# Where a weight conversion keeps its low word, and when half of a folded matrix leaves PSUM

## Chip, cores and metric

The kernel runs on one core of a Trainium2 chip. The metric is device microseconds (us) of one execution, as the median of three runs. TensorE multiplies matrices into PSUM (8 banks), VectorE and ScalarE work on SBUF and PSUM, GpSimd works on SBUF alone, and SyncE issues most DMAs. In the rows below PE is TensorE, DVE VectorE, ACT ScalarE, POOL GpSimd and SP SyncE.

## What is computed

Three stages in a row: an attention over keys and values that are pooled by 8, a bilinear layer with float64 weights, and a mixture of 8 experts with one expert for each token.

```python
k_p = k.reshape(B, H, Sp, pool, D).mean(axis=3)      # v_p likewise; pool = 8
attn = softmax(scale * q @ k_p.T);  x = attn @ v_p    # 4608 tokens x 512
a, b = x @ w1, x @ w2                                 # float64 weights, 512 x 1024
x = ((a * b) @ w3) @ w_out                            # 1024 x 1024, 1024 x 512
e = argmax(x @ w_gate + modality_bias[modality_id])   # one expert of 8
out = gate * relu(x @ ew1[e]) @ ew2[e]
```

## The kernel before

Every float32 matrix product is made of three passes over a high and a low part (`mm3`, lines 113 to 116). The float64 weights are loaded as raw 64-bit words, in pieces of 128x512 (512 KB), and turned into such a pair by `conv` (line 388). A conversion is a chain of six instructions. ScalarE makes two 32-bit words, the high one `m` (line 391) and the low one `t` (line 393), in the two halves of one SBUF tile `scr`. VectorE joins them in two operations (lines 394 and 395), each with both tensor inputs `m` and `t`. ScalarE rounds the result into the high part (line 396), and GpSimd subtracts that from it into the low part (`sub_pool`, line 119). There are 40 conversions: 24 for the fold, 16 for w1 and w2.

The **fold** computes w3 @ w_out once, as W (1024x512), in two passes of eight steps of 12 matmuls. The first pass takes a conversion of w_out and one of the first half of w3 for each step (16 in all), into four PSUM banks `accs` (the tag "mm"). The second takes one conversion a step, of the second half of w3, into `accs2`: the two banks of the tag "sc" and the two of the tag "tp". The first four attention tiles (`softmax_tile`, `attn_T`, `attn_V`, and `prep_v1` with the pooled values) run between the steps of the first pass. Then `fold_out` copies both halves out of PSUM as a high and a low part, on ScalarE (line 439) and VectorE (line 440), and `prep_w12(m)` converts piece m of w1 and w2. Pieces 0 and 1 come before the first chunk and pieces 2 to 7 in it, two conversions for each of the eight steps m of `mm1`, where attention tiles 4 to 7 run too. Their scores go to the tag "sc".

Values are summed by 8 in `pool_sum` (line 153), as one VectorE reduction (line 155) or as three additions on GpSimd (`tree_sum`, line 150). For batch 0, pieces 3 to 5 go to VectorE and pieces 0 to 2 to GpSimd; batch 1 is VectorE's; later batches are GpSimd's.

Raw pieces of the fold pass through a ring of 11 places. Places 0 to 3 lie in the SBUF of the tag "Wh" and places 4 to 7 in that of "Wl", so a tile of W in "Wh" cannot be written before the last conversion has read places 0 to 3. `fold_load` issues load n once conversion n - 11 is done.

The order of the work up to the end of the first chunk is made by the compiler's planner from the order in which the program is written and from its own estimate of when each instruction is ready. From the second chunk on the order is the written one. Each engine runs its own instructions in order.

Of the kernel before, what the change touches and what calls it, by code (L numbers as in the profile page):

```python
# [10 lines left out]
F32, F32R, BF16, I32, U32, I64, U16 = dt.float32, dt.float32r, dt.bfloat16, dt.int32, dt.uint32, dt.int64, dt.uint16  # L11
AF = mybir.ActivationFunctionType
ALU = mybir.AluOpType
# [9 lines left out]
P = 128  # L23
NT = N // P
NC_ = N // 512
SUM_V = (3, 4, 5)
IDC_M = 2
ACT_T, MM_T = (0, 1, 2, 4, 5, 6, 7), (1, 3)
V_POOL = 2
# [50 lines left out]
def flat(ap):  # L80
    return ap.rearrange("p a b -> p (a b)")
# [8 lines left out]
def _program(outer, tc, nc, I, out):  # L90
    def pool(stack, name, bufs=1, **kw):
        return stack.enter_context(tc.tile_pool(name=name, bufs=bufs, **kw))
# [3 lines left out]
    wp = pool(outer, "wp")  # L96
# [4 lines left out]
    def mm_ps(name, shape=(P, 512)):  # L101
        return psum.tile(list(shape), F32, name=name, tag="mm", bufs=4)

    def tp_ps(name, shape=(P, 512)):
        return psum.tile(list(shape), F32, name=name, tag="tp", bufs=2)

    def st4(name, shape, dtype):
        return st.tile(list(shape), dtype, name=name, tag="st4", bufs=6)

    def st2(name, shape=(P, 512), dtype=F32):  # L110
        return st.tile(list(shape), dtype, name=name, tag="st2", bufs=2)

    def mm3(ps, wh, wl, xh, xl, start, stop):
        nc.tensor.matmul(ps, lhsT=wh, rhs=xh, start=start, stop=False)  # L114
        nc.tensor.matmul(ps, lhsT=wh, rhs=xl, start=False, stop=False)  # L115
        nc.tensor.matmul(ps, lhsT=wl, rhs=xh, start=False, stop=stop)  # L116

    def sub_pool(lo, f, hi):
        nc.gpsimd.tensor_tensor(lo, f, hi.bitcast(F32), op=ALU.subtract)  # L119
# [28 lines left out]
    def tree_sum(out, t):  # L148
        for w in (4, 2, 1):
            nc.gpsimd.tensor_tensor(out if w == 1 else t[:, :, :w], t[:, :, 0] if w == 1 else t[:, :, :w],  # L150
                                    t[:, :, 1] if w == 1 else t[:, :, w:2 * w], op=ALU.add)

    def pool_sum(out, t, j, b):
        if 0 < b < V_POOL or b == 0 and j in SUM_V:
            nc.vector.tensor_reduce(out=out, in_=t, op=ALU.add, axis=AX.X)
            return
        tree_sum(out, t)
# [52 lines left out]
    def early_v(b):  # L210

        if b < B and b not in v_raw:
            pairs = [st4("vr2", (P, 2, D, POOL), F32) for _ in range(3)]
            v_raw[b] = [pairs[j // 2][:, j % 2] for j in range(6)]
            for j in range(6):
                load_v(b, j, v_raw[b][j])
# [167 lines left out]
    def load64(src, raw):  # L384
        nc.sync.dma_start(raw, src)
        return raw

    def conv(raw, hi, lo):
        s = st4("scr", (P, 2, 512), I32)
        f, m, t = s[:, 0].bitcast(F32), s[:, 0], s[:, 1]  # L390
        nc.scalar.activation(f, raw.bitcast(F32)[:, 1::2], AF.Copy, scale=float(2.0 ** -112))

        nc.scalar.activation(t, raw.bitcast(U32)[:, 0::2], AF.Copy, scale=TOP_S, bias=TOP_B)
        nc.vector.scalar_tensor_tensor(out=t, in0=m, scalar=3, in1=t, op0=ALU.logical_shift_left, op1=ALU.bitwise_or)
        nc.vector.scalar_tensor_tensor(out=m, in0=m, scalar=-2147483648, in1=t, op0=ALU.bitwise_and, op1=ALU.bitwise_or)
        nc.scalar.copy(hi, f)  # L396
        sub_pool(lo, f, hi)

    def run(hooks, n):
        for f in hooks.get(n, ()):  # L400
            f()
# [6 lines left out]
    ring = [x[:, i] for x in [wp.tile([P, 4, 512], I64, name="stage", tag=tag) for tag in ("Wh", "Wl")] for i in range(4)]  # L408
# [7 lines left out]
    order = [x for j in range(8) for x in (("wo", j), ("w3", j, 0))] + [("w3", j, 1) for j in range(8)]  # L416
    raws = {}

    def fold_load():
        n = len(raws)  # L420
        if n < len(order):
            k = order[n]
            raws[k] = load64(I[k[0]][k[1:]], ring[n % len(ring)])

    def fold_conv(k):
        dst = wos[k[1]] if k[0] == "wo" else w3s[k[1]]
        conv(raws[k], dst[:, 0], dst[:, 1])
        fold_load()

    def fold_mm(accs, j):  # L430
        w3, wo = w3s[j].rearrange("p t (k n) -> p t k n", k=4), wos[j]
        for k in range(4):
            mm3(accs[k], w3[:, 0, k], w3[:, 1, k], wo[:, 0], wo[:, 1], j == 0, j == 7)

    def fold_out(accs, h):

        for k in range(4):
            kb = 4 * h + k
            nc.scalar.copy(Wh[:, kb], accs[k])
            nc.vector.tensor_tensor(Wl[:, kb], accs[k], Wh[:, kb].bitcast(F32), op=ALU.subtract)  # L440

    names = ("w1h", "w1l", "w2h", "w2l")
    wt12 = []
    raw12 = {}
# [3 lines left out]
    def load_w12(m):  # L448
        if m < 8 and m not in raw12:
            raw12[m] = [load64(I[n][m], cv[:, 2 * (m % 2) + i]) for i, n in enumerate(("w1", "w2"))]  # L450

    def prep_w12(m):
        if m < 8 and m == len(wt12):
            load_w12(m)
            t = w12.tile([P, 4, 4, P], F32R, name=f"w{m}", tag=w_tag(m), bufs=1)
            wt12.append({n: t[:, i] for i, n in enumerate(names)})
            for i in range(2):
                conv(raw12[m][i], flat(t[:, 2 * i]), flat(t[:, 2 * i + 1]))
            load_w12(m + 2)

    att = Attention(0)
# [14 lines left out]
    accs = [mm_ps("wps") for _ in range(4)]  # L476
    for j in range(8):
        if j < 4:
            att.S(j)
        if j == 4:  # L480
            att.V1()
        if j == 5:
            sct = psum.tile([P, 2, 512], F32, name="sct", tag="sc", bufs=1)
            att.T((0, 1), {0: sct[:, 0], 1: sct[:, 1]})
            att.T((2, 3))
        if j == 6:
            sct = psum.tile([P, 2, 512], F32, name="sct", tag="sc", bufs=1)
            att.T((4,), {4: sct[:, 0], 5: sct[:, 1]})
        for k in order[2 * j:2 * j + 2]:
            fold_conv(k)  # L490
        fold_mm(accs, j)
    att.V()
    x_first = att.x
    sc = psum.tile([P, 2, 512], F32, name="wps3", tag="sc", bufs=1)
    accs2 = [sc[:, 0], sc[:, 1]] + [tp_ps("wps2") for _ in range(2)]
    load_w12(0)
    load_w12(1)
    for j in range(8):
        fold_conv(order[16 + j])
        fold_mm(accs2, j)  # L500
    prep_w12(0)
    Wh = wp.tile([P, 8, 512], F32R, name="Wh", tag="Wh")
    Wl = wp.tile([P, 8, 512], F32R, name="Wl", tag="Wl")
    fold_out(accs, 0)
    fold_out(accs2, 1)
    W = (Wh, Wl)
    prep_w12(1)


    def prep_routing():  # L510
# [44 lines left out]

    def mm_w(ch, ab, hooks, W, x2s, amid=None):
        abh, abl = ab
        Wh, Wl = W
        for i in range(4):
            t = 4 * ch + i  # L560
            cols = slice(P * i, P * i + P)
            ps = mm_ps("x2ps")
            for m in range(8):
                for l, r in ((abh, Wh), (abh, Wl), (abl, Wh)):
                    nc.tensor.matmul(ps, lhsT=l[:, m, cols], rhs=r[:, m], start=m == 0 and r is Wh and l is abh, stop=m == 7 and l is abl)  # L565
                if amid and i == 0 and m == 3:
                    amid()
            if i == 2:
                pair = st4("x2b", (P, 2, 512), F32)
            x2 = st2("x2") if i < 2 else pair[:, i - 2]  # L570
            nc.scalar.copy(x2, ps)
            nc.sync.dma_start(x2d[P * t:P * t + P, :], x2)
            x2s.append(x2)
            run(hooks, i)
# [67 lines left out]

    def first_chunk():
        att = Attention(1)
        h1 = {m: [lambda m=m: prep_w12(m + 2)] for m in range(8)}
        h1[0] += [lambda: att.K(0)]
        for i in range(4):
            h1[i + 1] += [lambda i=i: att.S(i)]
        h1[4] += [lambda: early_v(1)]
        h1[6] += [att.V1, lambda: att.T((0, 1))]  # L650
        h1[7] += [lambda: att.T((2, 3)), lambda: load_k(2), lambda: att.T((4,))]
        ab = mm1(0, x_first, h1)
        wgb = wp.tile([P, E, 512], F32, name="wgb", tag="wgb")
        nc.sync.dma_start(wgb, I["wgt"].partition_broadcast(P))
        return att, ab, wgb
# [4 lines left out]

    def next_chunk(ch, x, W, old):
        att = Attention(ch + 1)
# [8 lines left out]
        ab = mm1(ch, x, h1)  # L671
        mm_w(ch, ab, tail_hooks(ch, x2s, b, att), W, x2s)
        old_ent[:] = [sc[0][2]]
# [4 lines left out]
    x2s = []  # L678
    mm_w(0, ab, tail_hooks(0, x2s, 2, att1), W, x2s)
    x_cur = att1.x  # L680
    with tc.manual_schedule(engines={ET.PE, ET.DVE, ET.Activation, ET.Pool, ET.SP}):
        for ch in range(1, NC_ - 1):
            x_cur, x2s = next_chunk(ch, x_cur, W, x2s)
    def experts(x, old):
# [352 lines left out]
```

## Time and profile before

| | us |
|---|---|
| median of three runs (1221.94 to 1223.17) | 1222.15 |
| the profiled execution | 1223.66 |
| its span, first to last instruction | 1221.6 |
| TensorE busy in the span | 1166.5 |
| VectorE busy | 809.1 |
| ScalarE busy | 495.7 |
| GpSimd busy | 313.5 |

The profile was read in this order: the busy time of each engine, its slices in time, the waits of TensorE, and then the timelines of the other engines around those waits. An idle time in a row stands in brackets or behind the last bar, with what ended it. A busy TensorE is not one at full clock, so the granted clock (PEclk) is read beside it. A matmul's row is longer than its pitch, since neighbours overlap.

### The profile page before, as it was taken

Reading aid. Unit: us, or ns where it says so; the run is one execution under the profiler, and the core shown is the slowest. Engines: PE = TensorE matmul, PEld = TensorE weight load, DVE = VectorE, ACT = ScalarE, POOL = GpSimd, SP = SyncE. Lnnn points to the kernel's source line nnn. Section 1 sums busy time; section 2 is a strip of 40 time slices with the busy share of each in tenths; the row PEclk is TensorE's granted clock in tenths of the full one; section 3 lists DMA queues with packets and bytes.
Section 4 is the critical chain, followed back from the end, with each engine's and each line's share of the span. In section 5 each row is a group of like instructions: output and inputs, shape, how many; then the busy total and the mean of one; then the engine's idle time right before and its main releaser. Section 6 shows DMA issues by size and latency. Waiting matters only on the chain. (4 is left out here: it accounts for less than half of the span.)

```text
span 1221.6 us, 16215 instructions
## 1 busy us (share of the span) xinstructions
PE 1166.5 (95%) x5458; PEld 969.9 (79%) x5458; DVE 809.1 (66%) x1758; ACT 495.7 (41%) x967; POOL 313.5 (26%) x420
## 2 busy tenths in 40 slices
PE   4698899999999999999999999989999999999988
PEld 3466788888888888888888888868888888888867
DVE  6799787688687886877767684784444444445452
ACT  6587732222323223232232222713545545545452
POOL 3665501503315033150331101112121212122120
PEclk9899899999999999999999999989999999999998
DMA  9636332121121211211101000607645655654750
GB/s 334 205 139 221 133 114 72 48 76 43 57 91 48 73 45 56 91 48 71 47 18 36 1 35 17 217 10 266 182 129 182 192 144 172 208 156 131 203 149 18
DMA packets 89426, 136.68 MB, mean 112 GB/s; under 512 B 49304, under 2 KB 49560, under 8 KB 89176
## 3 DMA queue, kind: packets, MB, share of 16 engines
q1 hardware_dynamic: 82088, 115.72, 29.8%
q0 software_dynamic: 7232, 19.71, 5.0%
q8 instruction: 47, 0.77, 0.3%
q14 instruction: 59, 0.48, 0.1%
HBM read 106.26 MB, written 20.55 MB: 104 GB/s over the span
## 5 line engine op out<-in xcount | busy, mean ns | idle before, releaser
L114 PE MATMUL w<-xh,w 128*128 128x512 f32 x576 | 230.5, 400 | 3.7 <-ACT w L396 3.7
L116 PE MATMUL w<-xh,w 128*128 128x512 f32 x576 | 226.1, 392 | 1.4 <-POOL w L119 1.4
L115 PE MATMUL w<-xl,w 128*128 128x512 f32 x576 | 225.2, 391 | 0.0
L295 POOL TENSOR_TENSOR ex<-ex,sm 128x576 f32<-128x576 f32 x35 | 40.9, 1167 | 375.1 <-DVE sm L289 287.6
L114 PEld LDWEIGHTS w<-xh,w 128*128 128x128 f32 x576 | 108.9, 189 | 25.7 <-ACT w L396 4.1
L116 PEld LDWEIGHTS w<-xh,w 128*128 128x128 f32 x576 | 108.8, 189 | 25.8 <-POOL w L119 2.5
L115 PEld LDWEIGHTS w<-xl,w 128*128 128x128 f32 x576 | 109.0, 189 | 21.3
L764 DVE SCALAR_TENSOR_TENSOR abl<-e,abh 128x512 fp32r<-128x512 f32 (+2 forms) x80 | 51.8, 650 | 102.2 <-ACT abh L763 100.7
L114 PE MATMUL e<-e,abh 128*128 128x512 f32 x296 | 115.4, 390 | 0.5 <-ACT e L719 0.5
L115 PE MATMUL e<-e,abh 128*128 128x512 f32 x296 | 115.3, 390 | 0.2 <-DVE e L720 0.2
L116 PE MATMUL e<-e,abl 128*128 128x512 f32 x296 | 115.2, 389 | 0.0
L565 PE MATMUL x2ps<-Wh,abh 128*128 128x512 f32 x288 | 113.4, 394 | 0.8 <-DVE xl L324 0.8
L551 ACT CAST abh<-asb 128x512 fp32r<-128x512 f32 x72 | 44.7, 620 | 167.8 <-DVE asb L550 167.8
L565 PE MATMUL x2ps<-Wh,abl 128*128 128x512 f32 x288 | 112.4, 390 | 0.0
L565 PE MATMUL x2ps<-Wl,abh 128*128 128x512 f32 x288 | 112.3, 390 | 0.0
L777 POOL DMA_INDIRECT out<-o,idc x37 | 42.0, 1136 | 255.3 <-ACT o L776 143.0
L579 DVE CUSTOM_DVE_ANT_0 junk<-x2b,wgb,bias 128x512 f32<-128x512 f32 x144 | 102.3, 766 | 0.0
L579 DVE CUSTOM_DVE_ANT_0 junk<-x,wgb,bias 128x512 f32<-128x512 f32 x144 | 99.2, 755 | 0.2
L114 PE MATMUL e<-xh,e1h 128*128 128x512 f32 (+2 forms) x240 | 91.9, 383 | 5.6 <-DVEq L976 4.7
L550 DVE TENSOR_TENSOR asb<-asb,w 128x512 f32<-128x512 f32 x72 | 49.4, 685 | 66.2 <-PE w L116 31.1
L115 PE MATMUL e<-xl,e1h 128*128 128x512 f32 (+2 forms) x240 | 91.3, 380 | 0.0
L116 PE MATMUL e<-xh,e1l 128*128 128x512 f32 (+2 forms) x240 | 91.2, 380 | 0.0
(209 smaller groups left out, 2323.8 us busy)
## 6 DMA issues: line engine op xcount, KB each, us to landing
raw<-ew_in SPq DMA_DIRECT2D x80, 512.0 KB
q<-q_in SPq DMA_DIRECT2D x36, 256.0 KB
cv<-w_in SPq DMA_DIRECT2D x16, 512.0 KB
kr<-k_in SPq DMA_DIRECT2D x28, 288.0 KB
vr<-v_in SPq DMA_DIRECT2D x28, 256.0 KB
stage<-w_in SPq DMA_DIRECT2D x12, 512.0 KB
x2d<-x SPq DMA_DIRECT2D x18, 256.0 KB
x2d<-x2b SPq DMA_DIRECT2D x18, 256.0 KB
```

The source lines that it names most:

```text
L114: nc.tensor.matmul(ps, lhsT=wh, rhs=xh, start=start, stop=False)
L115: nc.tensor.matmul(ps, lhsT=wh, rhs=xl, start=False, stop=False)
L116: nc.tensor.matmul(ps, lhsT=wl, rhs=xh, start=False, stop=stop)
L295: eng.tensor_tensor(e3, e3, bc(sm.unsqueeze(2), [P, H, SP_]), op=ALU.mult)
L550: nc.vector.tensor_tensor(a, a, ps[1], op=ALU.mult)
L551: nc.scalar.copy(abh[:, m], a)
L565: nc.tensor.matmul(ps, lhsT=l[:, m, cols], rhs=r[:, m], start=m == 0 and r is Wh and l is abh, stop=m == 7 and l is abl)
L579: nc.vector.tensor_tensor_reduce(out=junk[e % 2], in0=x2s[i], in1=wgb[:, e], scale=1.0, scalar=bias[:, 4 * ch + i, e:e + 1], op0=ALU.mult, ...
L764: nc.vector.scalar_tensor_tensor(out=hT[1][:, m, :w], in0=ps[:, :w], scalar=0.0, in1=hT[0][:, m, :w].bitcast(F32), op0=ALU.max, op1=ALU.su ...
L777: nc.gpsimd.indirect_dma_start(out=out, out_offset=bass.IndirectOffsetOnAxis(idc[:, i, 0:1], 0), in_=o, in_offset=None, bounds_check=N - 1 ...
```

## The change

- `pool_sum` sends all six pieces of batch 0 to VectorE.
- `conv` takes `ps_of`, a maker of PSUM tiles. With it, the low word `t` lies in a PSUM bank and `m` stays in the SBUF tile. The fold's second pass uses it from step 2 on and `prep_w12(0)` and `prep_w12(1)` do, with the four "mm" banks; `prep_w12(2)` to `prep_w12(7)` use the two "tp" banks. That is 6 + 16 = 22 of the 40 conversions.
- `fold_out` for the first half (`accs`) runs in two parts behind steps 0 and 1 of the second pass, into a tile of its own in "Wh". The second half follows `prep_w12(1)`, into a tile in "Wl". W becomes a list of eight pairs.
- The last two raw loads of the fold (22 and 23) go to places 4 and 5 of the ring in place of 0 and 1, and are issued behind conversions 15 and 16 where they were behind 11 and 12.

```diff
     def pool_sum(out, t, j, b):
-        if 0 < b < V_POOL or b == 0 and j in SUM_V:
+        if b < V_POOL:
             nc.vector.tensor_reduce(out=out, in_=t, op=ALU.add, axis=AX.X)
...
-    def conv(raw, hi, lo):
-        s = st4("scr", (P, 2, 512), I32)
-        f, m, t = s[:, 0].bitcast(F32), s[:, 0], s[:, 1]
+    scr = []
+
+    def conv(raw, hi, lo, ps_of=None):
+        if len(scr) < 2:
+            s = st4("scr", (P, 2, 512), I32)
+            scr[:] = [s[:, 1], s[:, 0]]
+        m = scr.pop()
+        f, t = m.bitcast(F32), ps_of("low").bitcast(I32) if ps_of else scr.pop()
+        if len(scr) == 1 and not ps_of:
+            scr.clear()
...
-            raws[k] = load64(I[k[0]][k[1:]], ring[n % len(ring)])
+            raws[k] = load64(I[k[0]][k[1:]], ring[n % len(ring) if n < 22 else n - 18])
+
+    convs = []
...
-        conv(raws[k], dst[:, 0], dst[:, 1])
-        fold_load()
+        conv(raws[k], dst[:, 0], dst[:, 1], ps_of)
+        convs.append(k)
+        if len(raws) < 22 or len(convs) >= len(raws) - 6:
+            fold_load()
...
-    def fold_out(accs, h):
-        for k in range(4):
-            kb = 4 * h + k
-            nc.scalar.copy(Wh[:, kb], accs[k])
-            nc.vector.tensor_tensor(Wl[:, kb], accs[k], Wh[:, kb].bitcast(F32), op=ALU.subtract)
+    def fold_out(accs, w, ks):
+        for k in ks:
+            nc.scalar.copy(w[:, 0, k], accs[k])
+            nc.vector.tensor_tensor(w[:, 1, k], accs[k], w[:, 0, k].bitcast(F32), op=ALU.subtract)
+            W.append((w[:, 0, k], w[:, 1, k]))
...
+    W = []
+    w0 = wp.tile([P, 2, 4, 512], F32R, name="W0", tag="Wh")
...
     for j in range(8):
-        fold_conv(order[16 + j])
+        fold_conv(order[16 + j], mm_ps if j > 1 else None)
         fold_mm(accs2, j)
-    prep_w12(0)
-    Wh = wp.tile([P, 8, 512], F32R, name="Wh", tag="Wh")
-    Wl = wp.tile([P, 8, 512], F32R, name="Wl", tag="Wl")
-    fold_out(accs, 0)
-    fold_out(accs2, 1)
-    W = (Wh, Wl)
-    prep_w12(1)
+        if j < 2:
+            fold_out(accs, w0, (2 * j, 2 * j + 1))
+    prep_w12(0, mm_ps)
+    prep_w12(1, mm_ps)
+    fold_out(accs2, wp.tile([P, 2, 4, 512], F32R, name="W1", tag="Wl"), range(4))
...
-        h1 = {m: [lambda m=m: prep_w12(m + 2)] for m in range(8)}
+        h1 = {m: [lambda m=m: prep_w12(m + 2, tp_ps)] for m in range(8)}
```

## Rows read from the trace of the kernel before

**Rows 1.** Windows: stretch, length, then busy us of each engine (with counts), clock, DMA
```profile
155.00:1221.60 1066.60, 1048.59 (x4975) 879.28 (x4973) 683.94 (x1582) 388.61 (x696) 229.79 (x340) 0.99 0.32 99
```

**Rows 2.** Waits of PE, 15 to 155 us: total us, times, longest
```profile
PE wps L115 <- POOL f L119: 4.0, 1, 4.0
PE sc L265 <- ACT ex L280: 3.8, 1, 3.8
PE w L114 <- ACT w L396: 3.7, 1, 3.7
PE wps L116 <- POOL f L119: 3.4, 5, 1.3
PE w L116 <- POOL w L119: 1.4, 2, 0.9
```

**Rows 3.** Timeline of POOL, first pass: start, us, line, count, idle before
```profile
36.13 2.05 POOL L150 TENSOR_TENSOR earlyabl<-earlyabl 128x256 f32<-128x256 f32 x2
...
42.57 1.27 POOL L119 TENSOR_TENSOR f<-scr,f 128x512 fp32r<-128x512 f32 x1
```

**Rows 4.** Timelines of ACT and DVE, first pass
```profile
42.65 0.91 ACT L234 ACTIVATE vbh<-vs,c 128x256 fp32r<-128x256 f32 x2 [2.79 <-POOL vs L150]
...
54.80 0.59 ACT L305 CAST f<-sct 128x512 fp32r<-128x512 f32 x1 [5.48 <-PE sct L304]
...
43.19 1.33 DVE L235 SCALAR_TENSOR_TENSOR vbl<-vs,c,vbh 128x256 fp32r<-128x256 f32 x2 [1.68 <-ACT vbh L234]
...
55.42 0.69 DVE L306 TENSOR_TENSOR f<-sct,f 128x512 fp32r<-128x512 f32 x1 [2.63 <-ACT f L305]
```

**Rows 5.** Windows around three waits, and one without: columns PE, PEld, DVE, ACT, POOL, clock
```profile
43.90:52.70 8.80, 7.54 (x17) 5.47 (x18) 8.74 (x13) 4.69 (x10) 5.37 (x5) 0.51 0.70 243
77.00:94.00 17.00, 17.00 (x76) 14.07 (x75) 16.18 (x17) 13.85 (x26) 10.21 (x7) 1.00 0.28 85
106.80:110.40 3.60, 3.08 (x7) 2.03 (x8) 3.60 (x5) 3.60 (x8) 3.46 (x3) 0.55 0.03 14
125.70:131.30 5.60, 5.57 (x17) 4.86 (x18) 5.57 (x10) 4.55 (x9) 3.75 (x3) 0.52 0.26 91
```

**Rows 6.** Groups of DVE, 76.5 to 140 us: count, busy us, mean ns, idle before
```profile
L395 DVE SCALAR_TENSOR_TENSOR scr<-scr 128x512 int32<-128x512 int32 x21 | 20.9, 1008 | 0.2
L394 DVE SCALAR_TENSOR_TENSOR scr<-scr 128x512 int32<-128x512 int32 x21 | 20.4, 985 | 0.6 <-ACT scr L393 0.6
L440 DVE TENSOR_TENSOR Wl<-wps,Wh 128x512 fp32r<-128x512 f32 x8 | 5.0, 679 | 0.0
L552 DVE TENSOR_TENSOR abl<-asb,abh 128x512 fp32r<-128x512 f32 x4 | 3.6, 894 | 0.0
L550 DVE TENSOR_TENSOR asb<-asb,w 128x512 f32<-128x512 f32 x4 | 2.7, 676 | 0.0
L155 DVE TENSOR_REDUCE vs<-vr 128x64 f32<-128x512 f32 x4 | 2.7, 663 | 0.0
```

**Rows 7.** Groups of DVE, whole span: one that writes PSUM
```profile
L579 DVE CUSTOM_DVE_ANT_0 junk<-x,wgb,bias 128x512 f32<-128x512 f32 x144 | 99.2, 755 | 0.2
```

**Rows 8.** Timelines of POOL and DVE at one moment, pairs of instructions
```profile
96.13 3.35 POOL L119 TENSOR_TENSOR w<-scr,w 128x512 fp32r<-128x512 f32 x2 [4.84 <-ACT w L396]
...
96.57 3.46 DVE L395 SCALAR_TENSOR_TENSOR scr<-scr 128x512 int32<-128x512 int32 x2
```

**Rows 9.** Timelines of ACT and DVE: one low word from its start to its last reader
```profile
109.92 0.67 ACT L393 ACTIVATE scr<-cv 128x512 int32<-128x512 uint32 x1
...
113.95 1.79 DVE L395 SCALAR_TENSOR_TENSOR scr<-scr 128x512 int32<-128x512 int32 x2
```

**Rows 10.** Timelines of SP's queue and of ACT: raw loads, and the first reader
```profile
49.35 10.59 SPq L385 DMA_DIRECT2D stage<-w_in  x2
60.00 2.13 SPq L385 DMA_DIRECT2D cv<-w_in  x4
...
86.40 0.69 ACT L391 ACTIVATE scr<-cv 128x512 f32<-128x512 f32 x1
```

More of the change, by code (lines that the diff above doesn't have):

```diff
@@ L25 @@
 NC_ = N // 512
-SUM_V = (3, 4, 5)
 IDC_M = 2
@@ L422, in fold_load, with fold_conv @@
             k = order[n]
-            raws[k] = load64(I[k[0]][k[1:]], ring[n % len(ring)])
-    def fold_conv(k):
+            raws[k] = load64(I[k[0]][k[1:]], ring[n % len(ring) if n < 22 else n - 18])
+    convs = []
+    def fold_conv(k, ps_of=None):
         dst = wos[k[1]] if k[0] == "wo" else w3s[k[1]]
-        conv(raws[k], dst[:, 0], dst[:, 1])
-        fold_load()
+        conv(raws[k], dst[:, 0], dst[:, 1], ps_of)
+        convs.append(k)
+        if len(raws) < 22 or len(convs) >= len(raws) - 6:
+            fold_load()
     def fold_mm(accs, j):
@@ L450, in load_w12, with prep_w12 @@
             raw12[m] = [load64(I[n][m], cv[:, 2 * (m % 2) + i]) for i, n in enumerate(("w1", "w2"))]
-    def prep_w12(m):
+    def prep_w12(m, ps_of):
         if m < 8 and m == len(wt12):
@@ L457, in prep_w12 @@
             for i in range(2):
-                conv(raw12[m][i], flat(t[:, 2 * i]), flat(t[:, 2 * i + 1]))
+                conv(raw12[m][i], flat(t[:, 2 * i]), flat(t[:, 2 * i + 1]), ps_of)
             load_w12(m + 2)
@@ L557, in mm_w @@
         abh, abl = ab
-        Wh, Wl = W
         for i in range(4):
@@ L563, in mm_w @@
             for m in range(8):
-                for l, r in ((abh, Wh), (abh, Wl), (abl, Wh)):
-                    nc.tensor.matmul(ps, lhsT=l[:, m, cols], rhs=r[:, m], start=m == 0 and r is Wh and l is abh, stop=m == 7 and l is abl)
+                wh, wl = W[m]
+                for l, r in ((abh, wh), (abh, wl), (abl, wh)):
+                    nc.tensor.matmul(ps, lhsT=l[:, m, cols], rhs=r, start=m == 0 and r is wh and l is abh, stop=m == 7 and l is abl)
                 if amid and i == 0 and m == 3:
```

## The prediction, made before the run

> **What bounds the kernel now.** I read the windows first. From 155 us to the end TensorE is busy 1048.59 of 1066.60 us at a clock of 0.99 [rows 1]. Everything that the change touches lies before that, and behind it nothing but TensorE's own work sets the end. So a microsecond that TensorE gains before 155 us reaches the end whole, and one that another engine gains counts only where TensorE waited for it.
>
> TensorE's waits come second. Rows 2 show five lines out of the list for 15 to 155 us: 4.0 and 3.4 us in the fold for GpSimd's subtractions, 3.7 us for a cast of w1 or w2, 1.4 us for their subtractions, 3.8 us for a bank of scores. The reader should see that none of the five names VectorE, and then turn to the windows [rows 5]: around each wait VectorE is busy nearly all the time (8.74 of 8.80, 16.18 of 17.00, 3.60 of 3.60, 5.57 of 5.60 us). ScalarE, GpSimd and TensorE wait for each other, but VectorE is the stage of a conversion that has no time to spare. [...]
>
> The third view says why VectorE is full. Its two joins of a conversion take 1008 and 985 ns on average; the same shape with one operand in PSUM takes 676 to 679 ns [rows 6]. At 96 us two joins take 3.46 us while two subtractions of GpSimd take 3.35 us [rows 8]: the two engines hold each other up. Instructions with a PSUM operand do not show it (L550 676 ns), while L552, of the same shape with both inputs in SBUF, shows it too (894 ns) [rows 6].
>
> **Pooled values.** Three tree sums leave GpSimd; they ran from 36.13 to 42.57 us, with the fold's next subtraction right behind them at 42.57 [rows 3]. TensorE waited 4.0 us for that one, and up to 1.3 us for the next [rows 2]. Then it ran at clock 0.51: 17 matmuls in 8.80 us, of which up to 1.3 were waiting [rows 5]. Its pitch in the undisturbed window is 17.00/76 = 0.224 us, so 17 need 3.8 us and the excess is 8.8 - 1.3 - 3.8 = 3.7 us. TensorE's ceiling is thus 4.0 + 1.3 + 3.7 = 9.0 us. But that pass is fed by VectorE. It idled 1.68 us for the pooled values (through ScalarE's 2.79 us wait) and 2.63 us for a transpose that TensorE reached late (ScalarE's 5.48 us wait) [rows 4], 4.3 us together. It now takes three more reductions of 0.663 us, 2.0 us [rows 6]. That leaves 2.3 us, and joins that no longer meet the tree sums give perhaps one more; half of the 9.0 would need a VectorE that is free. I take **3.0 us** gained, ends 0 and 9.0.
>
> **Low word in PSUM.** The change covers 22 conversions, 44 joins; 42 joins lie in the window of rows 6, which is one conversion short. They take 41.3 us there. At 676 ns they would take 28.4, so VectorE gets 12.9 us back out of 63.5. None of it is TensorE's directly. What TensorE can gain is what it waited behind this backlog: 3.7 + 1.4 + 3.8 = 8.9 us [rows 2], plus the slow clock behind two of these. In 106.80 to 110.40, 7 matmuls should take 1.6 us; without the 0.5 us of the second L116 wait (1.4 less 0.9) they took 3.1, so 1.5 us excess. In 125.70 to 131.30 there are 17 instructions, 8 of them short score products; at about half clock some 2.5 of the 5.6 us are excess. Sum 8.9 + 4.0 = **12.9 us**. The 3.7 us wait has a second cause that goes too: the cast stood on ScalarE among the copies of the second half of W, which are now written behind it.
>
> What I do not expect back: the longest wait of L116, 0.9 us, is the first subtraction of w1 itself behind its cast, and the tiles and their order stay. So **12.0 us**.
>
> **Unknown costs of PSUM.** ScalarE has no row that writes PSUM. SBUF to SBUF takes 0.67 us [rows 9], PSUM to SBUF 0.59 [rows 4]; I take no change, with ends of plus or minus 22 x 0.08 = 1.8 us of ScalarE, which has idle time around every wait. VectorE's first join writes PSUM: between 676 ns [rows 6] and the 755 ns of another operation that writes PSUM [rows 7], up to 22 x 0.08 = 1.7 us off the 12.9. I take 676, the nearer operation.
>
> [...]
>
> **First half of W out earlier.** Four casts and four subtractions move from behind the second pass to its first two steps: 4 x 0.679 = 2.7 us of VectorE [rows 6] in a place where the joins of steps 0 and 1 are still in SBUF and feed TensorE step by step. Step 2's low word also needs a bank that these copies free. All of it on the path, with a slow clock behind it like the 1.5 us above, is 4.2; none is 0, since 2.7 us leave a later full stretch. I take **1.0 us** lost.
>
> **Queues.** SyncE waited in the last two fold loads from 49.35 to 59.94 and issued the loads of w1 and w2 behind them at 60.00; their first reader starts at 86.40 [rows 10]. If the planner keeps that order behind loads 22 and 23, which now follow conversions 15 and 16, they wait some 12 us longer and still have over 10 us. GpSimd issues no DMA here. Cost nothing; cover gone, each microsecond beyond it delays w1. The new tile in "Wh" needs ring places 0 to 3, read by conversion 14 of the first pass, so it adds no wait. The low words of w1 and w2 lie in banks that the first products of `mm1` reuse, but those products need the conversions' results anyway.
>
> **Sum.** 3.0 + 12.0 - 1.0 = 14.0 us. The profiled execution took 1223.66 (span 1221.6), so 1209.7 by its own measure; it stands 1.5 above the median 1222.15, from which the forecast is **1208**.
>
> **Rivals.**
> - *The collision stays* (the change does not do what it says): joins still read `m` from SBUF and hold up GpSimd. Against it speaks L550, which reads SBUF and PSUM and shows nothing. Then only the 3.0 us and part of the 3.7 us wait go: about 1217.
> - *Other limits take over*: VectorE is relieved, but the planner's new order makes ScalarE's casts or GpSimd's subtractions late in half the places. Then 3.0 + 6.0 - 1.0 = 8.0: 1214.
> - *Slower, by the two "tp" banks*: twelve conversions of the first chunk share them, and a bank is held from line 393 to the end of line 395. Before, that was 109.92 to 115.74, 5.8 us [rows 9]. Two conversions are wanted for each step of `mm1`, 24 matmuls at 0.224 = 5.4 us, and some 1 us of scores in four of them, about 6.1 on average. Up to 6.1 us of holding the banks cost nothing; beyond it each microsecond costs 6 (twelve conversions, two at a time), because ScalarE's queue stands at line 393 with the casts and the copies from TensorE's banks behind it. From 6.1 + 14/6 = 8.4 us on the kernel is slower than before; 9 us gives 1208 + 6 x 2.9 = 1225. For it: one join late in VectorE's queue holds both banks. Against it: 5.8 was with colliding joins.
> - *Everything comes back*: 9.0 + 12.9, 1200.
>
> **How the numbers follow.** Forecast (1203 to 1213) 0.54; half or collision (1213 to 1219.7) 0.20; all back 0.06; no change 0.08; slower by the banks, or by an order of the planner's that does likewise, 0.12. A measurement of this kernel tells about 0.2%, 2.4 us, from no change. The range 1201 to 1219 leaves out the slower and unchanged cases, which are 0.20. Faster 0.80, same 0.08, slower 0.12.
>
> **What would show it.** Right: joins from step 2 on near 0.68 us beside GpSimd's subtractions near 1.27; no tree sums at 36 us and TensorE's transposes some 3 us earlier; no 3.7 and 3.8 us waits behind the fold, and clock 1.00 there. Wrong: joins still at 1.0 us or more; ScalarE waiting at line 393 for VectorE; new waits in steps 1 to 3 of the second pass. The prediction fails if the planner moves the conversions so that TensorE waits elsewhere.

## The result, and the profile after

The changed kernel takes 1207.02 us (median of five runs, 1205.86 to 1209.5) beside 1222.55 for the kernel before in the same series (1221.94 to 1223.17 in five runs): a ratio of 0.988, 95% interval 0.987 to 0.9891. That is 15.5 us less; 1208 was forecast. The profiled execution took 1205.86 us, its span is 1203.8. It is the fastest of the five, and the one profiled before (1223.66) was slower than all five beside it, so the two profiles lie 17.8 us apart by their spans where the medians lie 15.5 apart.

Where the time went is read first from windows that are cut at three events on TensorE: the first product of the fold, its 97th (the first of the second pass) and the first product of w1; the last cut is the first product of W. Columns: stretch and length, then busy us (count) of PE, PEld, DVE, ACT and POOL, the granted clock, the DMA share and GB/s. First the kernel before, then the changed one:

```profile
15.31:73.47 58.16, 42.97 (x161) 30.56 (x161) 46.45 (x66) 41.28 (x110) 35.86 (x36) 0.85 0.73 255
73.47:96.30 22.83, 22.09 (x98) 17.96 (x97) 21.94 (x26) 19.51 (x36) 11.92 (x8) 1.00 0.29 90
96.30:160.30 64.00, 55.15 (x250) 44.55 (x248) 50.89 (x74) 41.72 (x122) 32.83 (x28) 0.92 0.44 151
```

```profile
14.80:68.95 54.15, 41.90 (x160) 30.50 (x161) 45.07 (x70) 41.35 (x111) 28.93 (x27) 0.87 0.73 256
68.95:93.40 24.45, 22.84 (x98) 17.74 (x97) 21.95 (x35) 21.10 (x39) 11.60 (x9) 1.00 0.46 160
93.40:144.10 50.70, 50.44 (x250) 41.89 (x248) 36.81 (x64) 39.06 (x119) 25.05 (x26) 1.00 0.53 177
```

The first pass is 4.0 us shorter, the second 1.6 us longer, and the first chunk up to its first product of W 13.3 us shorter, with the same 250 instructions on TensorE. There TensorE is now busy 50.44 of 50.70 us at clock 1.00; it was 55.15 of 64.00 at 0.92. The work behind the cut is what it was: 632.7 us from there to the first product of an expert (632.8 before) and 427.0 to the end (428.5).

The line numbers moved with the change: VectorE's joins are now lines 400 and 401, ScalarE's cast is 402, GpSimd's subtraction 118. `f` is a converted part for the fold, `w` one of w1 or w2, `wps` a bank of the fold and `sc` one of scores. The waits of TensorE from 15 to 145 us (total us, times, longest):

```profile
PE wps L113 <- ACT f L402: 8.4, 5, 2.8
PE wps L115 <- POOL f L118: 2.7, 5, 0.9
...
PE sc L264 <- ACT ex L279: 0.3, 1, 0.3
```

Of [rows 2], the 3.7 us wait for the cast of w1 or w2, the 1.4 us for their subtractions and the 4.0 us for a subtraction behind the tree sums are gone; the 3.8 us for a bank of scores is 0.3. What stays belongs to the fold. The first of these lines had a counterpart before that stood in no group, since the change was not expected to touch it:

```profile
PE wps L114 <- ACT f L396: 6.1, 5, 2.7
```

It grew by 2.3 us. 1.2 of them lie in the first pass, where GpSimd's two lines fell from 7.3 to 2.3: about a quarter of what the pooled values freed there is now waited for one step earlier in the same chain. The other 1.15 us is one new wait in the second pass, at 73 us, behind the early copies of W.

The joins from 0 to 165 us (groups of VectorE: count, busy us, mean ns, idle before), those with the low word in PSUM first, and GpSimd's subtractions of w1 and w2:

```profile
L400 DVE SCALAR_TENSOR_TENSOR low<-scr,low 128x512 int32<-128x512 int32 x22 | 14.9, 690 | 4.1 <-ACT low L399 4.0
L401 DVE SCALAR_TENSOR_TENSOR scr<-scr,low 128x512 int32<-128x512 int32 x22 | 14.4, 681 | 0.4
L401 DVE SCALAR_TENSOR_TENSOR scr<-scr 128x512 int32<-128x512 int32 x18 | 16.9, 950 | 0.3
L400 DVE SCALAR_TENSOR_TENSOR scr<-scr 128x512 int32<-128x512 int32 x18 | 14.4, 802 | 0.7 <-ACT scr L399 0.5
```

```profile
L118 POOL TENSOR_TENSOR w<-scr,w 128x512 fp32r<-128x512 f32 x16 | 20.5, 1295 | 19.2 <-ACT w L402 14.6 <-DVE W L448 3.7 <-DVE mx L276 0.8
```

690 and 681 ns with PSUM, 802 and 950 still in SBUF. The subtractions take 1295 ns. The same groups of the kernel before, over the same stretch:

```profile
L395 DVE SCALAR_TENSOR_TENSOR scr<-scr 128x512 int32<-128x512 int32 x40 | 38.9, 984 | 0.6
L394 DVE SCALAR_TENSOR_TENSOR scr<-scr 128x512 int32<-128x512 int32 x40 | 36.7, 929 | 2.7 <-ACT scr L393 2.5
```

```profile
L119 POOL TENSOR_TENSOR w<-scr,w 128x512 fp32r<-128x512 f32 x16 | 24.9, 1573 | 20.1 <-ACT w L396 17.6 <-issue 2.6
```

VectorE is no longer the stage that has no time to spare: from 77 to 140 us it is busy 50.03 of 63.00 us, and was 61.66 of 63.00.

### The profile page after: what moved, and what is told of

It is laid out like the page before. It is cut to its first block, busy times and chain, and to the rows that moved or that the text cites. A ratio compares the mean times of both kernels' runs of the same rounds, so it can differ in the third digit from the quotient of the medians.

```text
span 1203.8 us, 16217 instructions
## 1 busy us (share of the span) xinstructions
PE 1160.4 (96%) x5458; PEld 966.7 (80%) x5458; DVE 793.3 (66%) x1761; ACT 494.2 (41%) x967; POOL 298.1 (25%) x411
## 5 line engine op out<-in xcount | busy, mean ns | idle before, releaser
L574 PE MATMUL x2ps<-W,abh 128*128 128x512 f32 x576 | 179.0, 392 | 0.8 <-DVE xl L323 0.8
L574 PEld LDWEIGHTS x2ps<-W,abh 128*128 128x128 f32 x576 | 106.8, 188 | 22.3 <-DVE xl L323 1.2
L574 PE MATMUL x2ps<-W,abl 128*128 128x512 f32 x288 | 112.3, 390 | 0.0
L772 ACT ACTIVATE abh<-e 128x512 fp32r<-128x512 f32 (+2 forms) x80 | 45.0, 565 | 111.9 <-PE e L115 101.6
```

Source lines behind the costliest of these rows:

```text
L574: nc.tensor.matmul(ps, lhsT=l[:, m, cols], rhs=r, start=m == 0 and r is wh and l is abh, stop=m == 7 and l is abl)
L772: nc.scalar.activation(hT[0][:, m, :w], ps[:, :w], AF.Relu)
```

## The experiments

The theory is that of the prediction, **relief**: VectorE had no time to spare in the first chunk because its joins and GpSimd's subtractions hold each other up; PSUM takes the joins out of that, and TensorE's waits behind them go. The pooled values gain apart from it, in the first pass. Rivals: the gain comes from the new order alone; the two parts share one gain; it is not the collision that makes the joins long; two "tp" banks are about to bind.

The table gives the median, the time of the profiled execution, and stretches of that execution, cut as above, in us. Three profiled executions lie 2.4 to 3.1 us from their median, so a stretch is compared with the time beside it. In the four kernels in which the planner moves a whole step of the fold, the sum of the two passes alone is given.

| kernel | median | profiled | pass 1 | pass 2 | both passes | w1 to W |
|---|---|---|---|---|---|---|
| before | 1222.55 | 1223.66 | 58.2 | 22.8 | 81.0 | 64.0 |
| changed | 1207.02 | 1205.86 | 54.2 | 24.4 | 78.6 | 50.7 |
| sums only | 1219.81 | 1219.77 | 54.5 | 22.8 | 77.4 | 64.4 |
| all low words in SBUF | 1218.98 | 1222.12 | 54.6 | 24.7 | 79.3 | 63.1 |
| sums on GpSimd | 1210.73 | 1210.50 | 57.3 | 24.4 | 81.7 | 50.8 |
| low word in "tp" only | 1215.80 | 1215.80 | 57.6 | 22.8 | 80.5 | 57.9 |
| no subtraction | 1208.22 | 1208.22 | 53.0 | 21.8 | 74.8 | 54.5 |
| copies spread | 1207.40 | 1206.98 | 54.8 | 22.8 | 77.6 | 52.1 |
| V1 late | 1210.60 | 1213.04 | | | 82.7 | 50.9 |
| one "tp" bank | 1213.62 | 1213.53 | 55.5 | 24.2 | 79.7 | 53.6 |
| low word in "sc" | 1210.64 | 1211.60 | | | 82.5 | 50.2 |
| low word in "sc" and "tp" | 1214.81 | 1215.66 | | | 86.7 | 51.1 |
| subtractions on VectorE | 1209.35 | 1206.21 | | | 75.2 | 50.2 |

The start of the first product moves too (14.2 to 18.2 us), so both passes and it are read together where that matters.

### Sums only

The kernel before, with the pooled values of batch 0 on VectorE:

```diff
-SUM_V = (3, 4, 5)
+SUM_V = (0, 1, 2, 3, 4, 5)
```

> The kernel before with the three tree sums of batch 0 moved to VectorE and nothing else. Relief theory (VectorE's joins, freed of GpSimd by the PSUM word, carry most of the gain): 3 to 4 us faster than before, some 1219, joins still near 1.0 us behind the fold, and the waits of about 3.7 us behind it are still there. Rival (the whole gain starts in the first pass, and the rest follows from being earlier): 10 us or more, 1212 or less.

Measured: 1219.81 us beside 1222.25, ratio 0.9984 (0.9973 to 0.9995). Its waits of TensorE, 15 to 155 us:

```profile
PE sc L265 <- ACT ex L280: 4.3, 1, 4.3
PE w L114 <- ACT w L396: 2.8, 1, 2.8
```

The first pass is as short as in the changed kernel, 54.5, and behind the fold nothing changed, 64.4. So the pooled values are worth 2.4 us by the medians, and in the profile all of their gain lies in the first pass.

### All low words in SBUF

The changed kernel without its PSUM tiles, with its order, its early copies and its sums:

```diff
-        fold_conv(order[16 + j], mm_ps if j > 1 else None)
+        fold_conv(order[16 + j])
...
-    prep_w12(0, mm_ps)
-    prep_w12(1, mm_ps)
+    prep_w12(0, None)
+    prep_w12(1, None)
...
-        h1 = {m: [lambda m=m: prep_w12(m + 2, tp_ps)] for m in range(8)}
+        h1 = {m: [lambda m=m: prep_w12(m + 2, None)] for m in range(8)}
```

> The changed kernel with every low word back in SBUF; the pooled sums and the earlier copies of W's first half stay. Relief theory: the 13 us of the stretch from the first product of w1 to the first of W are lost, about 1219 to 1221, joins at 0.9 us or more. Rival (the new order of the copies of W is what frees the casts): still 1210 or less, with joins as slow as before.

Measured: 1218.98 us beside the kernel before, ratio 0.9972 (0.9963 to 0.9982), 12.0 above the changed kernel. Its joins, 0 to 165 us, and its waits of TensorE:

```profile
L401 DVE SCALAR_TENSOR_TENSOR scr<-scr 128x512 int32<-128x512 int32 x40 | 40.5, 1024 | 0.5
L400 DVE SCALAR_TENSOR_TENSOR scr<-scr 128x512 int32<-128x512 int32 x40 | 34.1, 861 | 1.0 <-ACT scr L399 0.7
```

```profile
PE sc L264 <- ACT ex L279: 3.5, 1, 3.5
PE w L113 <- ACT w L402: 2.8, 1, 2.8
```

With the joins long again, the same waits stand in the same places and the stretch from w1 to W is 63.1. So the written order and the early copies bring almost nothing there without PSUM. The planner's order is not held still by this edit: up to the first product of W, TensorE runs its instructions in the order of the changed kernel, but VectorE and ScalarE do not. That order alone is not the gain is shown below, under "No subtraction".

### Sums on GpSimd

The changed kernel with three pieces of batch 0 back on GpSimd:

```diff
-        if b < V_POOL:
+        if 0 < b < V_POOL or b == 0 and j in (3, 4, 5):
```

> The changed kernel with the three tree sums back on GpSimd. Relief theory with separate terms: 3 to 4 us slower than the changed kernel, 1210 to 1211, all of it before the second pass. Rival (the terms are one: with the sums on GpSimd the second pass starts late and VectorE catches up): less than 1 us apart, 1207 to 1208.

Measured: 1210.73 us, ratio 0.9908 (0.9892 to 0.9925), 3.7 more than the changed kernel. The 97th product of the fold comes at 72.43 us, where it came at 68.95, and w1 to W is the same:

```profile
72.43 0.40 PE L113 MATMUL wps<-f,f 128*128 128x512 f32 x1
```

Added or taken away, the pooled values are worth 2.4 to 3.7 us; that the two parts share one gain is refuted.

### Low word in the "tp" banks only

The kernel before, with PSUM for the low words of the twelve conversions in the first chunk and nothing else of the change:

```diff
-    def conv(raw, hi, lo):
+    def conv(raw, hi, lo, ps_of=None):
...
-        f, m, t = s[:, 0].bitcast(F32), s[:, 0], s[:, 1]
+        f, m, t = s[:, 0].bitcast(F32), s[:, 0], ps_of("low").bitcast(I32) if ps_of else s[:, 1]
...
-        h1 = {m: [lambda m=m: prep_w12(m + 2)] for m in range(8)}
+        h1 = {m: [lambda m=m: prep_w12(m + 2, tp_ps)] for m in range(8)}
```

> The kernel before with the low word in PSUM for pieces 2 to 7 of w1 and w2 alone, twelve conversions in the two tp banks; sums, copies of W and everything else as before. Relief theory: the waits behind scores and the slow clock there go (3.8 + 2.5 us), the waits at the fold's end stay, so 1215 to 1217. Rival (order of the copies of W): within 2 us of before, 1221 or more. Rival of the banks: slower than before.

Measured: 1215.80 us, ratio 0.9951 (0.9935 to 0.9966). Second joins of both kinds in one kernel, and what is left of TensorE's waits:

```profile
L395 DVE SCALAR_TENSOR_TENSOR scr<-scr 128x512 int32<-128x512 int32 x28 | 28.1, 1015 | 0.5
L395 DVE SCALAR_TENSOR_TENSOR scr<-scr,low 128x512 int32<-128x512 int32 x12 | 8.1, 682 | 0.5
```

```profile
PE w L114 <- ACT w L396: 2.9, 1, 2.9
```

In one kernel, 682 ns with PSUM beside 1015 without. The wait for a bank of scores, in the chunk, is gone; the wait for a cast of w1 or w2 stays. It comes at 104.85 us, in the second step of the chunk, and is for piece 1, which this kernel still converts in SBUF. w1 to W falls by 6.1 us, half of the changed kernel's 13.3.

### No subtraction

The kernel before; GpSimd writes zeros where it subtracted, so the low parts of the weights are left out and GpSimd reads nothing in a conversion:

```diff
-        sub_pool(lo, f, hi)
+        nc.gpsimd.memset(lo.bitcast(F32), 0.0)
```

> The kernel before, in which GpSimd does not subtract in the conversions: it fills the low part of the weights with zeros instead (the low part of w1, w2, w3 and w_out is left out of the result). Collision theory (GpSimd's reads of SBUF hold up VectorE's joins): joins of 0.68 to 0.75 us though both words are in SBUF, and the waits behind the fold go as with the PSUM word, some 10 us or more faster than before, 1212 or less. Rival (the joins are slow for another reason, such as two int32 words from SBUF): joins stay near 1.0 us and the time near 1219.

Measured in one run: 1208.22 us beside 1222.63. Joins with both words in SBUF, 0 to 165 us, and GpSimd's zeros:

```profile
L395 DVE SCALAR_TENSOR_TENSOR scr<-scr 128x512 int32<-128x512 int32 x40 | 28.0, 712 | 0.6
L394 DVE SCALAR_TENSOR_TENSOR scr<-scr 128x512 int32<-128x512 int32 x40 | 27.8, 705 | 3.0 <-ACT scr L393 2.7
L397 POOL MEMSET w<- 128x512 f32 x16 | 7.9, 529 | 10.1 <-PE wps L116 7.5 <-PE avps L116 2.6
```

The same instructions on the same tiles take 705 and 712 ns; with the subtractions they took 929 and 984. So the joins were long because of GpSimd's subtractions at the same time, and not by their own form. The zeros go to the same tiles and take 522 and 529 ns each, where the subtractions took 1491 and 1573; whether it is the reads of a subtraction or its length that holds the joins up was not separated. The kernel is almost as fast as the changed one. Up to the first product of W, TensorE, VectorE and ScalarE run the same instructions in the same order as in the kernel before, so no new order on these three engines has a part in the 14.4 us gained. Of the waits behind the fold, 2.2 us for a bank of scores is left. (Its time also lacks GpSimd's 1.3 us in each chain, so it is no price of the collision alone.)

### One "tp" bank

In the changed kernel a tile of 8 columns was to hold one of the two "tp" banks from the first step of the chunk to its seventh, by a write at the start and a read at the end. The first form was a plain copy as the reader:

```diff
+        hold = tp_ps("hold")
+        nc.vector.memset(hold[:, :8], 0.0)
...
-        h1[6] += [att.V1, lambda: att.T((0, 1))]
+        h1[6] += [lambda: nc.vector.tensor_copy(lg[:, 0], hold[:, :8]), att.V1, lambda: att.T((0, 1))]
```

> The changed kernel with one of the two tp banks held by a dummy from the start of the first chunk to its step 6, so that the twelve conversions there share one bank. Bank theory: a bank is held 2.2 to 7.6 us, some 4 on average, and two conversions a step of 6.1 us leave 3.05 each, so 12 x 1 = 10 us or more slower, 1217 or more, with ScalarE waiting at line 399 for VectorE. Rival (the planner hides it, the banks were never near a limit): within 2 us of the changed kernel.

Measured: 1206.69 us, ratio 0.9869 (0.9849 to 0.9889). Timeline of VectorE:

```profile
95.60 0.07 DVE L655 MEMSET hold<- 128x8 f32 x1
95.70 0.17 DVE L661 COPY lg<-hold 128x8 f32<-128x8 f32 x1
```

The planner put the reader right behind the writer, so the bank was held for 0.3 us. The run says nothing on banks; it repeats the changed kernel's time. In the second form the reader also needs the exponentials of the last tile, which come late:

```diff
-        h1[6] += [lambda: nc.vector.tensor_copy(lg[:, 0], hold[:, :8]), att.V1, lambda: att.T((0, 1))]
+        h1[6] += [lambda: nc.vector.tensor_tensor(lg[:, 0], hold[:, :8], att.ex[3][0][:, :8], op=ALU.add), att.V1, lambda: att.T((0, 1))]
```

> The changed kernel with one tp bank held through the first chunk up to the scores of its last tile, by a dummy whose reader waits for that tile's softmax, so that ten of the twelve conversions there share one bank. Bank theory: a bank is held 2.2 to 7.6 us, some 3.5 without a second conversion in flight, against 3.05 us that TensorE leaves for each; 10 x 0.5 to 10 x 1.5 us plus slow clock, 1212 to 1222. Rival (the low words never run two at a time where TensorE would notice): within 2.4 us of the changed kernel's 1207.

Measured: 1213.62 us, ratio 0.9925 (0.9908 to 0.9942), 6.6 more than the changed kernel; the bank was held from 96.9 to 140.4 us. Two low words (ScalarE's write, VectorE's last read, the next write), and waits of TensorE and ScalarE from 90 to 150 us:

```profile
98.83 0.64 ACT L399 ACTIVATE low<-cv 128x512 int32<-128x512 uint32 x1
100.30 0.69 DVE L401 SCALAR_TENSOR_TENSOR scr<-scr,low 128x512 int32<-128x512 int32 x1
101.55 0.62 ACT L399 ACTIVATE low<-cv 128x512 int32<-128x512 uint32 x1
```

```profile
PE w L115 <- POOL w L118: 1.9, 2, 1.2
...
ACT w L402 <- DVE scr L401: 8.5, 6, 2.9
```

With one bank each low word waits for the end of the one before, ScalarE waits 8.5 us for joins (0.8 in the changed kernel) and TensorE waits for subtractions of w1 and w2 again. So the mechanism of the rival "slower, by the two tp banks" exists. One bank less costs 6.6 us by the medians; in the profiles 2.9 us of the loss lie between w1 and W and 1.8 between there and the first product of an expert, while some 2 us lie ahead of the hold, in a start and a fold whose order is that of the changed kernel, so the bank's price is nearer to 4.7. With two banks the mechanism does not act. Counted in order, from ScalarE's write to the end of VectorE's second join, the twelve low words of the chunk are held 2.2 to 7.1 us, 4.3 on average. The longest pair, in the timelines of ScalarE and VectorE in the changed kernel:

```profile
117.92 1.31 ACT L399 ACTIVATE low<-cv 128x512 int32<-128x512 uint32 x2
...
124.29 1.28 DVE L401 SCALAR_TENSOR_TENSOR scr<-scr,low 128x512 int32<-128x512 int32 x2
```

It is held from 117.92 to 125.57, 7.6 us, and TensorE's one wait near it is the 0.3 us for a bank of scores.

### Copies spread

The changed kernel with the copies of W's first half at one pair for each of the steps 1 to 4, and PSUM low words from step 5 on:

```diff
-        fold_conv(order[16 + j], mm_ps if j > 1 else None)
+        fold_conv(order[16 + j], mm_ps if j > 4 else None)
...
-        if j < 2:
-            fold_out(accs, w0, (2 * j, 2 * j + 1))
+        if 0 < j < 5:
+            fold_out(accs, w0, (j - 1,))
```

> The changed kernel with the copies of W's first half spread over steps 1 to 4 of the second pass, one pair each, and the low word in PSUM from step 5 on. If the copies in front of the conversions cost the second pass its 1.6 us: up to 1.6 us faster than the changed kernel, 1205.5 to 1207. Rival (three more conversions with both words in SBUF cost as much): same or up to 1 us slower.

Measured: 1207.40 us, ratio 0.9875 (0.9859 to 0.9892), the same as the changed kernel. Its wait of TensorE in the first chunk:

```profile
PE sc L264 <- ACT ex L279: 1.3, 1, 1.3
```

The second pass gets its 1.7 us back (22.8), and w1 to W loses 1.4 (52.1), where the wait for a bank of scores returns with 1.3 us. Whether the three more conversions with both words in SBUF or the later copies bring it back was not separated.

### The first pass: three tries

In the first pass the joins are still long (802 and 950 ns on average for the 18 pairs in SBUF), and of the waits that TensorE has left nearly all lie in the fold. Three edits of the changed kernel try to take them. The first prepares the pooled values (`att.V1`, which calls `prep_v1`) two steps later:

```diff
-        if j == 4:
+        if j == 6:
```

> The changed kernel with the pooled sums of batch 0 written two steps later, in step 6 of the first pass in place of step 4. If the six reductions stand before the joins of step 4 and make TensorE's longest wait there (2.75 us and the slow clock behind it): 2 to 4 us faster than the changed kernel, 1203 to 1205. Rival (the attention's products then come late and hold the second pass): 1207 or more.

The second puts the low words of steps 3 and 4 of the first pass into the two halves of an "sc" tile:

```diff
+        low = []
+        if j in (3, 4):
+            sct = psum.tile([P, 2, 512], F32, name="lows", tag="sc", bufs=1)
+            low = [sct[:, 0], sct[:, 1]]
...
-            fold_conv(k)
+            fold_conv(k, (lambda _: low.pop()) if low else None)
```

> The changed kernel with the low words of the four conversions of steps 3 and 4 of the first pass in the two sc banks, which lie idle there between attention tiles. If the collisions that are left in the first pass cost TensorE time: four conversions x 0.39 us x 2 instructions' share, 1 to 3 us faster than the changed kernel, 1204 to 1206. Rival (the sc banks are wanted by the transposes, or VectorE's order is what counts): 1207 or more.

The third adds the "tp" banks at step 7:

```diff
+            fold_conv(k, (lambda _: low.pop()) if low else tp_ps if j == 7 else None)
```

> As the kernel with low words of steps 3 and 4 in sc, and those of step 7 in the tp banks. If collisions count there as well: another 0.5 to 1.5 us, 1203 to 1205. Rival: the attention's products, which take turns in the tp banks, wait, 1207 or more.

Measured: 1210.60 us, ratio 0.9899 (0.9883 to 0.9916); 1210.64, ratio 0.9896 (0.9877 to 0.9914); 1214.81, ratio 0.9932 (0.9916 to 0.9949). None gains. By the medians all lose, the first two 3.6 us, though the range of the second (1208.23 to 1211.96) overlaps that of the changed kernel, and the profile of the first is of its slowest execution. First joins of the second kernel (the second ones take 668 ns), then the longest wait of TensorE in each of the three, in their order:

```profile
L400 DVE SCALAR_TENSOR_TENSOR lows<-scr,lows 128x512 int32<-128x512 int32 x4 | 2.7, 686 | 0.0
```

```profile
64.75 0.79 PE L113 MATMUL wps<-f,f 128*128 128x512 f32 x1 [4.73 <-ACT f L402]
```

```profile
64.83 0.79 PE L113 MATMUL wps<-f,f 128*128 128x512 f32 x1 [4.74 <-ACT f L402]
```

```profile
64.13 0.79 PE L113 MATMUL avps<-f,vbh 128*128 128x512 f32 x1 [5.76 <-DVE scr L401]
```

The first two kernels share no edit, yet have one wait of the same length at the same place. The second's joins did become short (686 ns) and its time rose all the same. What they also share is an order: in both the planner puts twelve products of the fold, which stand at 54 us in the changed kernel, ahead of attention's products at 48 to 50 us, and the long wait is that of the next step of the fold. So in this pass the order that the planner derives from an edit weighs more than the length of these joins; in the third a product of attention has to wait until joins free the "tp" banks.

### Subtractions on VectorE

The last way to take GpSimd out of the first pass: in the changed kernel VectorE subtracts for the 18 conversions whose words both lie in SBUF.

```diff
-        sub_pool(lo, f, hi)
+        if ps_of:
+            sub_pool(lo, f, hi)
+        else:
+            nc.vector.tensor_tensor(lo, f, hi.bitcast(F32), op=ALU.subtract)
```

> The changed kernel with the subtraction of the 18 conversions whose low word is still in SBUF on VectorE in place of GpSimd. They cannot collide any more, which gives back some 18 x 0.39 = 7 us of VectorE, and they cost 18 x 0.68 = 12 us of it. Relief theory (VectorE sets the pace of the first pass): 3 to 6 us slower than the changed kernel, 1210 to 1213. Rival (the way through GpSimd, 1.36 us and two handovers, sets the pace): faster, 1203 to 1206.

Measured: 1209.35 us, ratio 0.9894 (0.9878 to 0.9911). VectorE's subtractions and second joins, and TensorE's first product of the fold:

```profile
L406 DVE TENSOR_TENSOR f<-scr,f 128x512 fp32r<-128x512 f32 x18 | 12.8, 730 | 0.4
L401 DVE SCALAR_TENSOR_TENSOR scr<-scr 128x512 int32<-128x512 int32 x18 | 12.1, 687 | 0.1
```

```profile
18.16 0.79 PE L113 MATMUL wps<-f,f 128*128 128x512 f32 x1 [1.99 <-ACT f L402]
```

18 joins in SBUF now take 687 ns where they took 950, once more without GpSimd's subtraction. The fold begins 3.4 us later than in the changed kernel, because the planner puts score products ahead of it, and needs 3.4 us less for both passes; the first product of w1 comes at 93.3 us, in the changed kernel at 93.4. What the end would be with an early start could not be seen. By the medians the kernel is 2.3 us slower than the changed one, with ranges that overlap (1206.21 to 1210.67 and 1205.86 to 1209.5), between what the two theories expected. What sets the pace of the first pass stays open.

## Why the prediction was right

**Bound.** A microsecond gained before 155 us was to reach the end whole. The changed kernel reaches its first product of W 16.2 us earlier (144.1 for 160.3) and ends 17.8 us earlier by its span; the stretches behind W differ by 1.6 us in sum, about as much as runs of one kernel differ.

**Pooled values, 3.0 us.** In the profile the first pass gained 4.0, by the medians of the two experiments 2.4 and 3.7. The working's reason, that VectorE feeds the pass too, shows in the timelines of ScalarE and TensorE (idle time in brackets) at the place of the old 4.0 us wait:

```profile
39.55 0.62 ACT L402 CAST f<-scr 128x512 fp32r<-128x512 f32 x1 [0.70 <-DVE scr L401]
...
40.22 0.50 PE L113 MATMUL wps<-f,f 128*128 128x512 f32 x1 [2.75 <-ACT f L402]
```

GpSimd is no longer late, and TensorE waits 2.75 us for the cast ahead of it, which waited for a join of VectorE. The clock came back in part: from 40 to 53 us it is granted 0.74, and was 0.61. The forecast left out that ScalarE's line of 6.1 us, not among its rows, would take back 1.2 in this pass.

**Low word in PSUM, 12.0 us.** 13.3 in the profile, 12.0 by undoing it. From w1 to W, TensorE's idle time fell by 8.6 us (8.85 to 0.26) and its busy time for the same 250 instructions by 4.7 (55.15 to 50.44), where the sum had 8.0 and 4.0. The joins were to take 676 ns and take 690 and 681, from 985 and 1008 [rows 6]; of the three waits behind the backlog 0.3 us is left, and the slow clock of 0.55 and 0.52 [rows 5] went with them, to 1.00 from w1 to W. The 0.9 us that was to stay, the first subtraction of w1 behind its cast, is gone as well; with all low words in SBUF it is already 0.2, so the PSUM word is not what took most of it. The second cause named for the 3.7 us wait, the copies of W on ScalarE, did not show: with the copies moved and the words in SBUF TensorE waits 2.8 us for that cast and 1.2 for the subtraction behind it, before 3.7 and 0.5.

**The price of PSUM.** ScalarE's write of a low word takes 665 ns into PSUM and 666 into SBUF; no change was forecast. (The two groups read different tiles; from the same tile `cv` the write into SBUF took 680 ns before.)

```profile
L399 ACT ACTIVATE low<-cv 128x512 int32<-128x512 uint32 x16 | 10.3, 665 | 0.0
L399 ACT ACTIVATE scr<-stage 128x512 int32<-128x512 uint32 x15 | 10.0, 666 | 0.0
```

Both joins read the low word from PSUM and take 690 and 681 ns, against 705 and 712 for the same joins in SBUF beside zeros, and 689 and 684 of these from 76.5 to 140 us. So the word in PSUM costs VectorE nothing that these runs show. From [rows 6] alone that could not be told: the joins and L552 there, with both inputs in SBUF, were themselves lengthened by GpSimd. L552, 894 ns there, takes 685 with the subtractions gone.

**Early copies, 1.0 us lost.** The second pass is 1.6 us longer, here and with the sums on GpSimd, and takes 22.8 us without copies at its start. TensorE waits in it for a cast, and 0.5 us for the subtraction behind it; with the copies spread it waits for neither:

```profile
73.25 0.51 PE L113 MATMUL wps<-f,f 128*128 128x512 f32 x1 [1.15 <-ACT f L402]
```

Mechanism right, term 0.6 too small.

**Queues at nothing.** The loads of w1 and w2 might have come 12 us later; they did not move. SyncE's queue after (start, us, line, count):

```profile
60.29 0.33 SPq L384 DMA_DIRECT2D stage<-w_in  x1
60.67 1.97 SPq L384 DMA_DIRECT2D cv<-w_in  x4
63.64 0.33 SPq L384 DMA_DIRECT2D stage<-w_in  x1
```

The planner put them between loads 22 and 23, at 60.67 for 60.00 [rows 10]. The cost of nothing was right, the order named as its risk was not.

**Rivals.** "The collision stays" falls with the 690 and 681 ns, "other limits" with TensorE busy 50.44 of 50.70 us. The bank rival was not put to the test by the change itself: the mean hold of 4.3 us lies below the 6.1 that it allowed (its terms, 5.4 and half of 1, make 5.9; a step took 50.7 / 8 = 6.3). That one pair held for 7.6 us cost nothing does not refute a threshold for the mean. Its price before, 5.8 us, was misread: the joins that end at 115.74 [rows 9] belong, counted in order, to the low words before the one of 109.92, whose last reader is the first of these two, up to 120.36:

```profile
119.69 1.28 DVE L395 SCALAR_TENSOR_TENSOR scr<-scr 128x512 int32<-128x512 int32 x2
```

With joins that collide a low word was thus held for 10.4 us, and the margin hung on the joins getting short, which they did. The mechanism decides once one bank is gone.

**Sum.** 14.0 was forecast; the stretches give 4.0 + 13.3 - 1.6 = 15.7, and the fold began 0.5 us earlier. The terms were off by 1.0, 1.3 and 0.6 us in the profile; two gains were taken too small and so was the one loss, which offset part of that. By the medians the gain is 15.5. The range of 1201 to 1219 left out the 1200 of "everything comes back" as well as the slower and unchanged cases that the prediction named.

## What to carry to other kernels

Where VectorE and GpSimd both work on pairs of SBUF tiles, compare the mean of one shape with both inputs in SBUF and with one in PSUM: here 985 to 1008 against 676 ns of another operation told what the change would bring, and a free PSUM bank for one operand was the remedy, worth 12 us. Price it by the waits of TensorE behind the backlog, not by the 12.9 us of VectorE time that come back. Where a planner orders the work, an edit that shortens instructions can lose more by its new order than it gains, so each must be measured, and the order of the two traces compared: eight joins of the first pass brought down to some 0.68 us went with a loss of 3.6 us by the medians.

## What was unexpected

- A VectorE operation with an operand in PSUM is not slower here than one with both in SBUF, at 512 columns: 690 and 681 ns against 689 and 684, the latter from 76.5 to 140 us in the kernel whose conversions have no subtraction.
- GpSimd gained too: its subtractions of w1 and w2 went from 1573 to 1295 ns each, though their own operands did not move.
- The start moves with the first data: VectorE's first reduction, which waits for the first load of keys, began between 6.61 and 8.38 us in the fourteen profiles, though nothing ahead of it was edited. Stretches are better compared from an event on TensorE than from the start of the span.
